# Loads of a table and of raw weights moved behind a store, and fewer idle matmuls, in front of step B of an FFT and MLP kernel

## The chip, the cores and the metric

The kernel runs on one core of a Trainium2 chip. The metric is the device time of one execution in microseconds (us), as the median of several runs. A core has five engines that work at the same time and wait for one another by semaphores: TensorE (PE in the profile, PEld its weight loads), VectorE (DVE), ScalarE (ACT), GpSimd (POOL) and SyncE (SP). SP, ACT and POOL also issue transfers (DMA). An instruction queue is worked off in order, so an issue that waits holds up those behind it. Queue 1 of the DMA carries what SP issues, queue 0 what POOL issues, queue 10 what ACT issues; all of them run on the same 16 DMA engines.

## The reference

The input `x` is 4 batches of 3008 tokens with 256 channels. Each batch goes through a Fourier transform over the tokens, a complex 256 x 256 mix with bias, a soft threshold, and the inverse transform. All 12032 tokens then go through a layer of 2048 hidden units with a leaky ReLU of its own slope for each unit.

```python
X = np.fft.rfft(x, axis=1)
Yr = Xr @ w_r - Xi @ w_i + b_r
Yi = Xr @ w_i + Xi @ w_r + b_i
Yr = np.sign(Yr) * np.maximum(np.abs(Yr) - lam, 0.0)
Yi = np.sign(Yi) * np.maximum(np.abs(Yi) - lam, 0.0)
y = np.fft.irfft(Yr + 1j * Yi, n=3008, axis=1)
...
h = y.reshape(12032, 256) @ w_in
g = np.maximum(h, 0.0) + alpha * np.minimum(h, 0.0)
return (g @ w_out).astype(np.float32)
```

`w_in` and `w_out` come as 64-bit floats. The kernel loads their raw words and converts each number on the chip into a high and a low 32-bit part (the `conv` steps).

## The kernel before

The transform of 3008 = 47 x 64 points is split. **Step A** (`a_load`, `a_mm`, `a_evac`) does the 47-point transforms as matmuls with the table `lf_s`: 16 groups `g` to a batch, two of them to a load. For batch 0 the result stays in SBUF as `a0_s`; for later batches `a_evac` copies it to a staging tile `ast` and puts a store to the DRAM buffer `ad` on a list, which `put()` issues on SP. **Step B** (`b_load`, `b_mm`, `b_evac`) takes the 24 slots of the first frequency index in 12 pairs `q`. `b_load(q)` rearranges pair `q` into a tile `bt` (three buffers); for batch 0 it copies from SBUF to SBUF by two transfers on POOL's queue. `b_mm(q)` multiplies with slots 2q and 2q+1 of the table `rb_s`. **The mix** (`m_mm`, `m_evac`) multiplies with the mixing weights `wr_s` and `wi_s`, **step C** (`c_mm`, `c_evac`) does the inverse 64-point part and stores to the buffer `zd`, and **step D** (`d_load`, `d_step`) the inverse 47-point part. What step D gives goes into the layer's two products (`l1_step`, `l2_step`, later `s_l1`, `s_l2`).

Nothing moves instructions but the program itself: each engine and each queue does its work in the order in which the code calls it (`tc.manual_schedule()`), and semaphores are set between engines where data or a buffer is passed on.

Batch 0's steps A to D stand alone at the start, up to about 104 us; there is no other work for TensorE yet. The steps of batches 1 to 3 are woven into the layer's products later. At the start SP issues, in order: batch 0's input (`x`), slots 0 to 3 of `rb_s`, the first input of batch 1 (`xt`), the mixing weights (`wm_f`), slots 4 to 11 of `rb_s`, and two loads of raw expert weights (`conv_load`, into `cw_s`). A loop over `seq` then does step A for batch 0's 16 groups and for batch 1's first 4 (the variable `EARLY`). In it, at `n == NG` (behind batch 0's last group), POOL is given `b_load` for q = 0, 1 and 2 (six transfers) and then `split_mix`: ScalarE writes the high parts of the mixing weights, and POOL behind its six issues the low parts (L142). Behind the loop come `put()`, which issues the four stores of batch 1's groups on SP, two small loads (`rd_s`, `alpha_s`), and `keep_warm(WARM)`: matmuls on a tile of zeros whose results nobody reads.

The loop over `t` then runs step B, the mix and step C in a pipeline. In round `t` TensorE has `b_mm(t)`, `m_mm(t-1)` and `c_mm(t-3)`; POOL has `b_load(t+3)`, which needs `b_mm(t)` to have freed the buffer, then the two negations of `X(t)` (L450, in `b_evac2`), which the `wi_s` matmuls of `m_mm(t)` read. `pump(PT[t])` puts in so many steps of the conversion of the raw weights. `m_evac(0)` writes its first result into the buffer `Yc`, one of the four in which batch 1's first groups wait for their stores.

Of the kernel before, what the change touches and what calls it, by code (L numbers as in the profile page):

```python
# [93 lines left out]
def fft_mix_moe(ctx, tc, x, w_r, w_i, b_r, b_i, w_in, w_out, alpha, la, rb, lc, rd, lf, cf, sel, out):  # L94
# [72 lines left out]
    def half(h):  # L167
        t = const.tile([128, 2, FH * 2 * C], F32R, tag=f"half{h}", name=f"w{h}")
        wi_h[h] = t[:, 0].rearrange("p (w k f) -> p w k f", w=2, k=CT)
        wo_h[h] = t[:, 1].rearrange("p (m w f) -> p m w f", w=2, f=C)  # L170

    def load_tables():
        nc.sync.dma_start(out=rd_s, in_=rd)
        nc.sync.dma_start(out=alpha_s, in_=alpha.rearrange("(k p) -> p k", p=128))
# [31 lines left out]
    def load_mix(*tags):  # L206
        for w, tag in zip((w_r, w_i), tags):
            t = work.tile([128, CT, C], F32, tag=tag, name="wm_f", bufs=1 if tag[1] in "tc" else None)
            nc.sync.dma_start(out=t, in_=w.rearrange("(k p) f -> p k f", p=128))
            mix_w.append(t)  # L210

    def load_rb(n0, n1):
        nc.sync.dma_start(out=rb_s[:, n0:n1], in_=rb[:, n0:n1])
# [10 lines left out]
    def split_mix():  # L224
        for t, w in zip(mix_w, mix):
            split(t, w[:, 0], w[:, 1], A, G)
        mix_w.clear()
# [24 lines left out]
    def conv_load():  # L252

        m, i = divmod(conv_m[0], 2)
        conv_m[0] += 1
        k = conv_m[0] % 3
        raw = cw_s[:, NSLOT + 8 * k:NSLOT + 8 * k + 8].rearrange("p (k n) f -> p k (n f)", k=2)
        raw = raw.rearrange("p k (n w) -> p k n w", w=2)
        src = w_out.bitcast(U32)[256 * m:256 * m + 256] if i else w_in.bitcast(U32)[:, 512 * m:512 * m + 512]
        nc.sync.dma_start(out=raw.rearrange("p k n w -> p k (n w)"), in_=src.rearrange("(k p) f -> p k f", p=128))  # L260
        conv_raw.append((raw, m, i))
# [48 lines left out]
    def pump(n):  # L310

        while n > 0:
            if not conv_ops:
                conv_fetch()
                second = conv_second(*conv_old.pop()) if conv_old else []
                first = conv_first(*conv_raw.pop(0)) if conv_raw else []
                first, second = ([(op,) for op in ops] for ops in (first, second))
                if first and second:
                    conv_ops.extend([second[0] + first[0], first[1], second[1], second[2] + second[3] + first[2]])
                else:  # L320
                    conv_ops.extend(first + second)
                if not conv_ops:
                    return
            for op in conv_ops.pop(0):
                op()
            n -= 1
# [5 lines left out]
    def put(*queues):  # L332
        for n, (o, i) in enumerate(stores):
            (queues or (nc.sync,))[n % max(len(queues), 1)].dma_start(out=o, in_=i)
        stores.clear()
# [44 lines left out]
    def a_mm(b, g):  # L380
        ps = ps_f.tile([NQ, 2, C], F32, tag="f", name="ps_a")
        pa[b, g] = ps
        if b < 2:
            ts = x_rows(b, g)
            n = 2 // len(ts)
            for i, t in enumerate(ts):
                PE.matmul(ps[:, n * i:n * i + n], lf_s, t, start=True, stop=True)  # L387
            return
        hi, lo = xp.pop((b, g))
        PE.matmul(ps, la_s[:, 0], hi, start=True, stop=False)  # L390
        PE.matmul(ps, la_s[:, 1], hi, start=False, stop=False)
        PE.matmul(ps, la_s[:, 0], lo, start=False, stop=True)

    def a_evac(b, g):
        ps = pa.pop((b, g))
        if b == 0:
            st = a0_s[:, g]
        else:
            tag = A1_TAGS[g] if b == 1 and g < len(A1_TAGS) else "zst"
            st = work.tile([NQ, 2, C], F32, tag=tag, name="ast", bufs={"bt": 3, "Yt": 1, "Yc": 1}.get(tag))  # L400
        if b == 0 and g % 2:
            V.tensor_copy(out=st, in_=ps)
        else:
            A.activation(out=st, in_=ps, func=AF.Copy)
        if b:
            stores.append((ad[b][:, 2 * g:2 * g + 2], st))
# [3 lines left out]
    def b_load(b, q):  # L410
        t = work.tile([128, 2, C], F32, tag="bt", name="bt", bufs=3)
        if b == 0:
            src = a0_s.rearrange("(w s q) g r c -> q w s (g r) c", w=4, s=2)[q]
        else:
            src = ad[b].rearrange("(w s q) r c -> q w s r c", w=4, s=2)[q]

        for k in range(2):
            (nc.gpsimd if b == 0 else nc.sync).dma_start(out=t[:, k], in_=src[:, k])
        bt[b, q] = t
# [546 lines left out]
    NG = R // 2  # L966
    EARLY = 4
    FILL = 14
    C0 = 2
    PT = [1, 2, 3, 3, 3, 3, 3, 3, 3, 3, 4, 4]  # L970
    TAIL = [['f', 1], ['ce', 3], ['me', 1], ['cm', 2], ['f', 1], ['ce', 2], ['cm', 1], ['ce', 1], ['d'], ['f', 2], ['e'], ['f', 6]]
    WARM = 70
    A1_TAGS = ("zst", "zst", "Yt", "Yc", "bt", "bt", "bt", "Xh", "Xl", "Xh", "Xl", "zst", "zst", "Yc")
    X1_TAGS = {4: ("Yl", "Yl"), 5: ("os", "Yt"), 6: ("gh",) * 4}
    idle = const.tile([128, 128], BF16, name="idle")
# [1 line left out]
    def keep_warm(n):  # L977
        ps = ps_f.tile([128, 512], F32, tag="f", name="ps_idle")
        for _ in range(n):
            PE.matmul(ps[:, 0:128], idle, idle, start=True, stop=True)  # L980

    with tc.manual_schedule():
# [8 lines left out]
        for g in range(EARLY // 2):  # L991
            a_load(1, g)
        load_mix("Yh", "Yh")
        load_rb(4, 12)
        conv_tags.update(v1=("yh", "yl"), ex=("xh", "xh"), lf=("xl", "xl"))
        for _ in range(C0):
            conv_load()
        seq = [(0, g) for g in range(NG)] + [(1, g) for g in range(EARLY)]

        for n, (b, g) in enumerate(seq):  # L1000
            a_mm(b, g)
            if n >= 1:
                a_evac(*seq[n - 1])
            if n == NG:
                for q in range(3):
                    b_load(0, q)
                split_mix()
                bias_parts()
        a_evac(*seq[-1])
        half(0)  # L1010
        put()
        load_tables()
        keep_warm(WARM)

# [13 lines left out]
        for t in range(NPAIR + 1):  # L1028
# [8 lines left out]
            if t < NPAIR:  # L1037
                pump(PT[min(t, len(PT) - 1)])
            if t in (2, 5):
# [152 lines left out]
        for k in range(len(spairs) + SLAG):  # L1192
# [9 lines left out]
            if k >= SLAG:  # L1202
                n, t = spairs[k - SLAG]
# [43 lines left out]
```

## Time and profile before

| what | value |
|---|---|
| time, median of 3 runs | 1356.6 us (1356.08 to 1357.65) |
| time of the profiled execution | 1356.09 us |
| its span (first to last instruction) | 1354.3 us |
| TensorE busy | 1339.6 us, 99% of the span |
| VectorE, ScalarE, POOL busy | 1037.7, 759.2, 379.5 us |
| chain that ended last | 96% on TensorE, 1% each on VectorE, ScalarE and DMA |

The span leaves out 1.8 us of the execution around the instructions. Busy time is a sum over the whole span; where an engine waits is seen in its timeline alone, which gives the start, the length and, in brackets, the idle time ahead of an instruction with what ended it. A row of a timeline merges like instructions that follow each other (xcount).

### The profile page before, as it was taken

The page shows a single profiled execution, that of the slowest core. Times are in us where ns is not written, and L with a number is a line of the kernel's source. Part 1 is how long each engine was busy: PE and PEld are TensorE (multiplying, and loading weights), DVE is VectorE, ACT ScalarE, POOL GpSimd, SP SyncE. Part 2 cuts the span into 40 slices and gives each one's busy share as a digit, 9 for nine tenths or more (in the row PEclk, how much of TensorE's full clock was granted, in tenths as well). Part 3 has the DMA queues.
Part 4 walks back from the last instruction along what each step waited for, and adds up shares of the span by engine and source line. Part 5 has one row for each costly group of instructions (what it writes and reads, how often), then busy time and mean ns, then how long its engine had stood idle before and what let it go on. Part 6 is the DMA issues. An engine that isn't in the chain of part 4 may idle for free.

```text
span 1354.3 us, 25104 instructions
## 1 busy us (share of the span) xinstructions
PE 1339.6 (99%) x9208; PEld 1252.3 (92%) x9208; DVE 1037.7 (77%) x1931; ACT 759.2 (56%) x1528; POOL 379.5 (28%) x403
## 2 busy tenths in 40 slices
PE   9999999999999999999999999999999999999998
PEld 5979989999999999999999999999999999999998
DVE  2766866777777777776768888888888888888885
ACT  3566645665566655545556555555565556555553
POOL 3854742221322232222212211122112111221222
PEclk9999999999999999999999999999999999999999
DMA  9964223342334312111110110111011101110001
GB/s 238 261 173 152 82 94 98 103 136 85 97 97 129 98 64 81 45 59 47 36 36 1 40 28 2 39 28 27 6 36 28 28 6 36 29 28 8 21 17 28
DMA packets 88119, 89.66 MB, mean 66 GB/s; under 512 B 42318, under 2 KB 70449, under 8 KB 87996
## 3 DMA queue, kind: packets, MB, share of 16 engines
q1 hardware_dynamic: 79428, 76.76, 19.9%
q0 software_dynamic: 5168, 8.02, 2.3%
q10 hardware_dynamic: 3399, 3.27, 0.8%
q8 instruction: 73, 1.20, 0.4%
q14 instruction: 51, 0.41, 0.1%
HBM read 50.49 MB, written 34.34 MB: 63 GB/s over the span
## 4 chain that ended last, share of the span: by engine, by line
PE 96%; DVE 1%; DMA 1%; issue 1%; ACT 1%; POOL 0%; ACTq 0%; DVEq 0%
PE ps_h L785 24%; PE ps_h L680 14%; PE ps_m L486 6%; PE ps_o L887 6%; PE ps_o L888 6%; PE ps_o L886 6%; PE ps_d L611 4%; PE ps_o L718 3%; PE ps_o L717 3%; PE ps_o L719 3%; PE ps_b L426 3%; PE ps_m L473 3%; PE ps_a L387 2%; PE o_last L719 2%; PE o_last L717 2%; PE o_last L718 2%
## 5 line engine op out<-in xcount | busy, mean ns | idle before, releaser
L785 PE MATMUL ps_h<-yh,w 128*128 128x512 f32 (+1 forms) x960 | 315.6, 390 | 0.0
L824 POOL TENSOR_TENSOR l<-t,h 128x512 fp32r<-128x512 f32 x98 | 127.0, 1296 | 496.6 <-ACT h L822 456.7
L785 PEld LDWEIGHTS ps_h<-yh,w 128*128 128x128 f32 x960 | 180.0, 188 | 33.2
L789 DVE SCALAR_TENSOR_TENSOR sq<-sq,beta_s,ps_h 128x512 f32<-128x512 f32 (+1 forms) x240 | 168.0, 733 | 55.0 <-ACT sq L788 54.2
L680 PE MATMUL ps_h<-yh,w 128*128 128x384 f32 (+1 forms) x704 | 206.2, 335 | 2.7 <-DVE q L687 2.7
L785 PE MATMUL ps_h<-yl,w 128*128 128x512 f32 (+1 forms) x480 | 186.3, 388 | 0.0
L691 ACT ACTIVATE gh<-q 128x384 fp32r<-128x384 f32 (+1 forms) x192 | 99.1, 516 | 148.6 <-DVE q L687 147.5
L687 DVE SCALAR_TENSOR_TENSOR q<-q,beta_s,ps_h 128x384 f32<-128x384 f32 (+1 forms) x192 | 115.5, 601 | 79.9 <-ACT q L686 78.1
L692 POOL TENSOR_TENSOR gl<-q,gh 128x384 fp32r<-128x384 f32 (+1 forms) x90 | 96.6, 1073 | 267.0 <-ACT gh L691 259.5
L804 ACT ACTIVATE dh<-sq 128x768 fp32r<-128x768 f32 x112 | 94.8, 846 | 118.0 <-DVE sq L789 72.8
L788 ACT ACTIVATE sq<-ps_h 128x512 f32<-128x512 f32 (+1 forms) x240 | 133.1, 586 | 27.5 <-PE ps_h L785 23.0
L680 PEld LDWEIGHTS ps_h<-yh,w 128*128 128x128 f32 x704 | 129.3, 189 | 5.7 <-DVE q L687 2.2
L822 ACT ACTIVATE h<-t 128x512 fp32r<-128x512 f32 x98 | 62.0, 633 | 104.5 <-DVE t L820 101.2
L680 PE MATMUL ps_h<-yl,w 128*128 128x384 f32 (+1 forms) x352 | 116.5, 331 | 0.0
L686 ACT ACTIVATE q<-ps_h 128x384 f32<-128x384 f32 (+1 forms) x192 | 91.4, 476 | 35.5 <-PE ps_h L680 34.2
L719 PE MATMUL ps_o<-w,gl 128*128 128x256 f32 x384 | 107.9, 281 | 1.7 <-POOL gl L692 1.7
L718 PE MATMUL ps_o<-w,gh 128*128 128x256 f32 x384 | 108.3, 282 | 0.0
L717 PE MATMUL ps_o<-w,gh 128*128 128x256 f32 x384 | 107.9, 281 | 0.0
L785 PEld LDWEIGHTS ps_h<-yl,w 128*128 128x128 f32 x480 | 90.5, 189 | 13.6
L819 DVE TENSOR_TENSOR dl<-sq,dh 128x768 fp32r<-128x768 f32 x98 | 93.4, 954 | 3.8 <-ACT dh L804 3.6
L888 PE MATMUL ps_o<-l,sw_a 128*128 128x256 f32 x294 | 82.0, 279 | 0.0
L886 PE MATMUL ps_o<-h,sw_a 128*128 128x256 f32 x294 | 81.9, 279 | 0.0
(211 smaller groups left out, 3625.6 us busy)
## 6 DMA issues: line engine op xcount, KB each, us to landing
zt<-zd SPq DMA_DIRECT2D x32, 384.0 KB
ad<-ast SPq DMA_DIRECT2D x48, 192.0 KB
bt<-ad SPq DMA_DIRECT2D x72, 128.0 KB
zd<-zst SPq DMA_DIRECT2D x36, 256.0 KB
xt<-in_x SPq DMA_DIRECT2D x21, 320.0 KB
out<-oT SPq DMA_DIRECT2D x152, 32.0 KB
cw_s<-in_moe_w_in SPq DMA_DIRECT2D x8, 512.0 KB
cw_s<-in_moe_w_out SPq DMA_DIRECT2D x8, 512.0 KB
```

What stands on the lines that cost most here:

```text
L680: PE.matmul(ps, wi_h[m // FH][:, w, ct, 128 * (m % FH):128 * (m % FH) + 128], a[:, ct, 0:n], start=(k == 0), stop=(k == 3 * CT - 1))
L687: V.scalar_tensor_tensor(out=q, in0=q, scalar=beta_s[:, m:m + 1], in1=ps, op0=ALU.mult, op1=ALU.add)
L691: A.activation(out=hi, in_=q, func=AF.Copy)
L717: PE.matmul(a, hi[:, t], w[:, 0], start=(i, k) in first, stop=False)
L718: PE.matmul(a, hi[:, t], w[:, 1], start=False, stop=False)
L719: PE.matmul(a, lo[:, t], w[:, 0], start=False, stop=(i, k) in last)
L785: PE.matmul(ps, wi_h[m // FH][:, w, ct, 128 * (m % FH):128 * (m % FH) + 128], a[:, ct, 0:w1], start=(k == 0), stop=(k == 3 * CT - 1))
L788: A.activation(out=q[:, j], in_=ps, func=AF.Relu, scale=-1.0)
L789: V.scalar_tensor_tensor(out=q[:, j], in0=q[:, j], scalar=beta_s[:, m:m + 1], in1=ps, op0=ALU.mult, op1=ALU.add)
L824: G.tensor_tensor(out=l24, in0=t24, in1=f(h24), op=ALU.subtract)
L886: PE.matmul(o, wh, gh, start=first, stop=False)
L888: PE.matmul(o, wh, gl, start=False, stop=last)
```

## The change

Three loads leave their place on SP ahead of step A's loop. At `n == NG + 1`, when batch 1's group 0 is on the list of stores, `put()` now issues this one store; behind it stand the first raw load, slots 4 to 11 of the table, and the second raw load. `WARM` falls from 70 to 20, and the first round of step B puts in no step of the conversion (`PT[0]` from 1 to 0).

```diff
-    PT = [1, 2, 3, 3, 3, 3, 3, 3, 3, 3, 4, 4]
+    PT = [0, 2, 3, 3, 3, 3, 3, 3, 3, 3, 4, 4]
...
-    WARM = 70
+    WARM = 20
...
         load_mix("Yh", "Yh")
-        load_rb(4, 12)
         conv_tags.update(v1=("yh", "yl"), ex=("xh", "xh"), lf=("xl", "xl"))
-        for _ in range(C0):
-            conv_load()
         seq = [(0, g) for g in range(NG)] + [(1, g) for g in range(EARLY)]
 
         for n, (b, g) in enumerate(seq):
...
                 split_mix()
                 bias_parts()
+            if n == NG + 1:
+                put()
+                conv_load()
+                load_rb(4, 12)
+                for _ in range(C0 - 1):
+                    conv_load()
         a_evac(*seq[-1])
```

On SP, from the mixing weights (`wm_f`) on, the issues stand as follows; a row with - stands there before alone, one with + after alone.

```order
 L209 DMA wm_f<-in_w_r 128x2x256
 L209 DMA wm_f<-in_w_i 128x2x256
+L334 DMA ad_158<-ast 96x512
+L260 DMA cw_s<-in_moe_w_in 128x2x512
 L213 DMA rb_s<-tab_rb 128x1024
-L260 DMA cw_s<-in_moe_w_in 128x2x512
-L260 DMA cw_s<-in_moe_w_out 128x2x512
-L334 DMA ad_158<-ast 96x512 x4
+L260 DMA cw_s<-in_moe_w_out 128x2x512
+L334 DMA ad_158<-ast 96x512 x3
```

The table's slots and the two raw loads (`cw_s`) went from the place behind the mixing weights to the place behind the first of the four stores (`ad`); the other three stores, `rd_s` and `alpha_s` have three transfers more ahead of them than before.

On ScalarE, from the second split of a mixing weight to the second round of step B, there stood before (`Xh` is `b_evac`'s copy, L273 a conversion's first step, L499 is in `m_evac(0)`):

```order
L139 ACTIVATE wi_s<-wm_f 128x512
L404 ACTIVATE ast<-ps_a 96x512 x4
L440 ACTIVATE Xh<-ps_b 128x4x128
L273 ACTIVATE conv<-cw_s 128x512
L440 ACTIVATE Xh<-ps_b 128x4x128 x2
L499 ACTIVATE Yc<-ps_m,lam_s 128x512
L273 ACTIVATE conv<-cw_s 128x512
```

and there stands now:

```order
L139 ACTIVATE wi_s<-wm_f 128x512
L404 ACTIVATE ast<-ps_a 96x512 x4
L440 ACTIVATE Xh<-ps_b 128x4x128 x2
L273 ACTIVATE conv<-cw_s 128x512
L440 ACTIVATE Xh<-ps_b 128x4x128
L499 ACTIVATE Yc<-ps_m,lam_s 128x512
L273 ACTIVATE conv<-cw_s 128x512
```

The first step of the conversion, which reads the first raw load, went from between the first two `Xh` copies to behind both, and the steps that follow it are each a little later in the rounds.

## Rows read from the trace of the kernel before

**Rows 1.** Chain that ended last, 20 to 105 us: start us, us, what
```profile
20.99 2.08 POOL bt L418 x3
...
23.07 8.02 DMA bt<-a
...
31.14 0.71 PE ps_b L426 x4
...
32.28 3.05 PE ps_m L473 x24
...
104.12 0.93 PE ps_d L611 x8
```

**Rows 2.** TensorE's timeline: start us, us, engine line op out<-in form xcount
```profile
1.00 4.02 PE L980 MATMUL ps_idle<-idle 128*128 128x128 bf16 x36 [1.00 <-DVE idle L986]
...
23.29 1.10 PE L387 MATMUL ps_a<-xt,lf_s 94*96 94x512 f32 x2 [1.11 <-ACT ast L404]
...
24.23 4.07 PE L980 MATMUL ps_idle<-idle 128*128 128x128 bf16 x70
...
29.46 2.38 PE L426 MATMUL ps_b<-rb_s,bt 128*128 128x128 f32 x16 [1.17 <-issue]
...
33.02 0.40 PE L473 MATMUL ps_m<-wi_s,Xh 128*128 128x256 f32 x2
...
33.26 0.28 PE L473 MATMUL ps_m<-wi_s,Xl 128*128 128x256 f32 x1
...
35.16 1.06 PE L426 MATMUL ps_b<-rb_s,bt 128*128 128x128 f32 x8
...
44.77 1.05 PE L426 MATMUL ps_b<-rb_s,bt 128*128 128x128 f32 x8
```

**Rows 3.** Timeline of all engines, POOL's rows (a row merges neighbours)
```profile
20.99 4.10 POOL L418 DMA_DIRECT2D bt<-a  x6 [15.91 <-DVE bias_h L199]
...
26.42 1.26 POOL L142 TENSOR_TENSOR wi_s<-wm_f,wi_s 128x512 fp32r<-128x512 f32 x1
...
30.89 1.37 POOL L418 DMA_DIRECT2D bt<-a  x2 [3.21 <-PE ps_b L426]
...
32.29 0.41 POOL L450 TENSOR_SCALAR Xh<-Xh 128x256 fp32r<-128x256 f32 x1
...
32.66 0.41 POOL L450 TENSOR_SCALAR Xl<-Xl 128x256 fp32r<-128x256 f32 x1
...
33.66 1.37 POOL L418 DMA_DIRECT2D bt<-a  x2
```

**Rows 4.** `bt`'s issue at 20.99 on POOL, time to landing
```profile
DMA to landing us min/median/max: 8.4/8.4/8.4
```

**Rows 5.** DMA queues, 22 to 23 us: packets, MB, share of 16 engines
```profile
q1 hardware_dynamic: 165, 0.40, 101.7%
```

**Rows 6.** DMA queues, 25 to 26 us
```profile
q0 software_dynamic: 156, 0.18, 99.9%
...
q1 hardware_dynamic: 54, 0.09, 28.5%
```

**Rows 7.** Timeline of all engines, ScalarE's first split of a mixing weight
```profile
21.40 0.63 ACT L139 ACTIVATE wr_s<-wm_f 128x512 fp32r<-128x512 f32 x1 [2.03 <-DMA wm_f<-in_w_r]
```

**Rows 8.** SP's queue, timeline of its issues
```profile
16.77 0.38 SPq L213 DMA_DIRECT2D rb_s<-tab_rb  x1
...
18.98 0.37 SPq L260 DMA_DIRECT2D cw_s<-in_moe_w_out  x1
...
23.26 5.42 SPq L334 DMA_DIRECT2D ad<-ast  x4
```

**Rows 9.** DMA issues, 1 to 2 us: KB each, median us to landing
```profile
lf_s<-tab_lf POOLq DMA_DIRECT2D x1, 35.2 KB, 2.8
```

**Rows 10.** SP's queue, 25 to 26.5 us
```profile
24.43 2.31 SPq L334 DMA_DIRECT2D ad<-ast  x1
```

**Rows 11.** `bt`'s issues from 33.66 on, time to landing
```profile
DMA to landing us min/median/max: 9.6/10.0/10.3
```

## The prediction

> **What bounds the kernel now.** I read the page first: TensorE is busy nearly all of the span, so a change saves time only where TensorE stands still or does work that is not wanted. Then I read the chain of work that ended last, in order of time, around the edit [rows 1]. There the reader is to see that TensorE is not the link between step A and step B. The chain goes from the third `bt` issue on POOL's queue into a transfer that takes 8.02 us, lands at 31.09, and releases the second half of `b_mm(1)` at 31.14. From there to the end of step B, and on through the fill work to step D's first matmul at 104.12, the chain lies on TensorE almost without a break. So about 8 us ahead of step B are set by a transfer, and all later work hangs on it.
>
> TensorE's timeline shows the same from its side [rows 2]. Step A ends at 24.39. The 70 idle matmuls run from 24.23 to 28.30. `b_mm(0)` starts at 29.46, so there is a hole of 1.17 us even behind the idle matmuls. The idle matmuls are therefore no cost of their own: they fill a wait for `bt`.
>
> Why is `bt` late? By its landing row the first transfer takes 8.4 us from its issue at 20.99 [rows 3, 4], so it lands at 29.4, just ahead of `b_mm(0)`. The queue rows show what the engines did instead. Between 22 and 23 us queue 1 (SP's) has 101.7% of the 16 DMA engines and moves 0.40 MB, and queue 0 (POOL's, which carries `bt`) has no row at all [rows 5]. Between 25 and 26 us queue 0 has 99.9% and queue 1 is down to 28.5% [rows 6]. What queue 1 carries from about 21.4 on is known from the order of SP's issues: `w_r`'s load released ScalarE at 21.40 [rows 7], and behind the two mixing loads stand slots 4 to 11 of the table (issued at 16.77) and two raw weight loads, the last issued at 18.98 [rows 8]. Each of the three is 128 x 1024 words of 4 bytes, 1.57 MB together. At 0.40 MB in 1 us they are 3.9 us of all DMA engines: the stretch from 21.4 to about 25.
>
> **The change, part by part.**
>
> *Three transfers go behind the first store.* They now stand on SP behind the store of (1, 0), which SP issues at 23.26 [rows 8], as it waits for ScalarE's copy of that group. ScalarE's copies, TensorE's matmuls of step A and the issues on POOL stand as before. All six `bt` issues lie on POOL between 20.99 and 25.09 [rows 3], and the four of `bt(0)` and `bt(1)` are ahead of the first moved transfer. So the 3.9 us of foreign work in front of them go. Estimate: `bt(0)` lands at 29.4 - 3.9 = 25.5, the second half of `bt(1)` at 31.1 - 3.9 = 27.2. The bounds: nothing (if `bt` is slow by itself), and, from the other side, the 2.8 us that the small load of `lf_s`, POOL's first, took from issue to landing [rows 9]; that would put `bt(0)` at 24 to 24.5. I take the middle one, since the queue rows show the very stretch.
>
> *50 idle matmuls fewer.* 4.07 us for 70 is 0.058 us each, so the 20 that stay end at about 28.30 - 2.9 = 25.4. This alone gains nothing, for `b_mm(0)` waited until 29.46; but with 70 it could not have started before 28.3. Together the two edits let `b_mm(0)` start at about 25.5, 3.9 us earlier.
>
> *What is late next.* The stall goes to POOL. Its queue is in order: six `bt` issues, the two low parts of the mixing weights until 26.42 + 1.26 = 27.68, then `bt(3)`'s two issues (1.37 us), then the two negations of `X(0)` [rows 3]. In the trace `bt(3)` starts at 30.89, when `b_mm(0)` has freed its buffer. After the change it can start at 27.68 and no earlier: 3.21 us gained, not 3.9. The negated halves are used by the `wi_s` matmuls of `m_mm(0)`. The high half was ready at 32.70 for a matmul at 33.02 (0.32 us of slack), the low half at 33.07 for one at 33.26 (0.19 us) [rows 2, 3]. TensorE may use up the smaller slack, so these matmuls move by 3.21 + 0.19 = 3.4 us. From there TensorE runs without a gap into `b_mm(2)`, from 35.16 to 31.8.
>
> *Costs at nothing, and their covers.* `b_mm(2)` needs the moved table slots, now due at 31.8. Issued behind the store and one raw load at about 24.5, they have 1.25 MB to go through queue 1, store, raw load and themselves (96 x 512, 128 x 1024 and 128 x 1024 words); at 0.40 MB per us that needs 3.1 us of engines shared with `bt(2)`; I expect them at 29 to 31. One us of cover is thin. The first raw load is wanted by ScalarE's conversion, whose first step now stands behind the second `Xh` and not between the first two; the next ScalarE operation for which TensorE waits is `Xh(2)`, 4 us later, so a late raw load costs nothing below that. The conversion is one of its steps behind at the end of step B, and the drain of the tail carries that step out while TensorE has fill work until step D. The other three stores, `rd`, `alpha` and the third raw load on SP get later by the three transfers that now stand ahead; the store out of `Yc` must land before ScalarE overwrites that buffer in `m_evac(0)`, and ScalarE has 3 us or more there before `Xh(3)`.
>
> *Sum.* The profiled execution took 1356.1 us; minus 3.4 is 1352.7. It ran 0.5 us under the median of the three runs (1356.6), so the median of the changed kernel should be 1353.2, 0.25% less.
>
> **A rule against it.** The Trainium skill, "DMA: Bandwidth & Descriptors", section "Queues, rings and completion order", says that each DMA engine goes round robin between the queues that have work for it, a packet at a time. By that rule queue 0 would have had its turns from 22 us on whatever queue 1 held, and moving queue 1's work would help little; what that would give is rival 3. The row of 22 to 23 us shows no packet of queue 0 beside a full queue 1, so here the trace does not bear the rule out for the start of a transfer; in the row of 25 to 26 both move.
>
> **The rivals.**
>
> 1. *The table comes late.* For it: while `bt` flows, an issue on SP can take 2.31 us [rows 10] where others take 0.38 [rows 8]. If store, raw load and table each take that, the table's issue ends at 23.26 + 3 x 2.31 = 30.2; its data takes 1.3 us at 0.40 MB per us and twice to three times that if it shares the engines, so it lands at 31.5 to 34, up to 2.2 us behind 31.8. The gain shrinks to between 1.2 and 2.7 us: 1353.9 to 1355.4 on the median's scale, on which the rivals below stand too. Against it: the long issues end when `bt` is through, and that is earlier now.
>
> 2. *The gain is given back in step B.* `bt(4)` was the tightest transfer of the step: its second half took 10.3 us from its issue at 34.34 (two issues of 0.68 us from 33.66), landed at 44.65 and was used at 44.77 [rows 2, 11]. Its issue now comes some 3.2 us earlier. If the DMA engines have the same work ahead of it as before, it lands at 44.6 again, and 3.3 of the 3.4 us are lost: 1356.5. Against it: most of what stood ahead of it on queue 1 (`alpha`, the third raw load, the next slots) is issued later relative to it.
>
> 3. *The change does not free `bt`.* Later `bt` transfers take long too. If the first ones take 8.4 us for themselves, `b_mm(0)` stays at 29.46 and nothing is gained. TensorE would then stand still from 25.4 on for 4 us. The first idle matmuls, which follow on nothing, took 4.02 us for 36, 0.112 us each [rows 2], twice the 0.058 of the later ones: by their length the lower of the two levels of the clock, 1.2 of 2.4 GHz. If the clock falls in the hole, a like stretch of 4 us at the lower level loses 2 us: 1356.6 to 1358.6. Against it: the row with queue 1 alone.
>
> 4. *The table comes so late that the kernel is slower.* It decides from a landing at 35.2, where `b_mm(2)` stood. If the issue comes at 30.2, as in rival 1, and the landing takes 8.4 us as `bt`'s did, `b_mm(2)` starts at 38.6, 3.4 us later than before: 1360.0. Against it: behind 30 us there is far less ahead of it in the queues than was ahead of `bt` at 21.
>
> **How the numbers follow.** A measurement of this kernel can tell some 0.2%, 2.7 us, from no change. The forecast (2.7 to 4 us gained) has 0.52, rival 1 0.18, rival 2 0.14, rival 3 0.08, rival 4 0.08. The forecast's own range is 1352.6 to 1353.9. Faster is the forecast alone, 0.52; same is rivals 1 and 2 and most of rival 3, 0.39; slower is rival 4 and a little of 3, 0.09. The range runs from 1352.0 (all 3.9 us gained against the profiled execution's own 1356.1, and 0.2 of scatter) to 1356.8, which takes in rivals 1 and 2 and leaves out 3 and 4.
>
> **What would show it.** Right: the first `bt` lands within 5 us of its issue; `b_mm(0)` starts near 25.5; `bt(3)` starts on POOL at 27.7; the `wi_s` matmuls of `m_mm(0)` are near 29.6 and wait for POOL; `b_mm(2)` is near 31.8; step D starts near 100.7. Wrong: `b_mm(0)` near 29 (rival 3); a wait of `b_mm(2)` for `rb_s` (1 and 4); a wait of `b_mm(4)` or a later one for `bt` (2). The forecast is wrong if step D starts less than 2.7 us earlier.

## The result, and the profile after

| | before | after |
|---|---|---|
| median, us (range) | 1356.34 (1355.21 to 1357.65, 6 runs) | 1364.35 (1362.52 to 1368.46, 5 runs) |
| ratio to before, 95% interval | 1 | 1.0060 [1.0048, 1.0071] |
| profiled execution, us; its span | 1356.1; 1354.3 | 1363.2; 1361.5 |
| end of step A; first matmul of step D, us | 24.39; 103.96 | 24.97; 111.11 |
| step D to the end of the span, us | 1250.3 | 1250.4 |

The changed kernel is slower by 8 us; 3.4 us faster was forecast. A sixth run of after, 1455.17 us at a granted clock of 0.849, is left out, here and in the ratio; with it the median is 1365.33. From step D on the two profiled executions take the same time, so in them all of the loss lies between 24 and 111 us.

TensorE's timeline of the kernel after, to be read against [rows 2]:

```profile
24.81 1.28 PE L980 MATMUL ps_idle<-idle 128*128 128x128 bf16 x20
25.93 1.11 PE L426 MATMUL ps_b<-rb_s,bt 128*128 128x128 f32 x8
28.34 0.68 PE L426 MATMUL ps_b<-rb_s,bt 128*128 128x128 f32 x4 [1.30 <-DMA bt<-a]
30.30 0.71 PE L426 MATMUL ps_b<-rb_s,bt 128*128 128x128 f32 x4 [1.28 <-DMA bt<-a]
...
32.70 0.63 PE L473 MATMUL ps_m<-wi_s,Xh 128*128 128x256 f32 x2
...
35.85 1.06 PE L426 MATMUL ps_b<-rb_s,bt 128*128 128x128 f32 x8
...
43.62 0.50 PE L466 MATMUL ps_m<-bias_p,ones 4*128 4x512 f32 x1 [2.34 <-DVE Y L500]
...
92.82 0.50 PE L466 MATMUL ps_m<-bias_p,ones 4*128 4x512 f32 x1 [1.44 <-DVE Y L500]
...
111.11 3.89 PE L611 MATMUL ps_d<-rd_s,zt 96*128 96x94 f32 x32
```

The reader is to see three things. `b_mm(0)` does start 3.5 us earlier (25.93 for 29.46). The gain is gone at once: `b_mm(1)` waits twice for its own `bt`, the pair of `wi_s` and `Xh` takes 0.63 us where it took 0.40, and `b_mm(2)` is at 35.85, where it was at 35.16. And two waits follow that the prediction did not have, ahead of 43.62 and of 92.82.

The granted clock by stretches, in the kernel after (columns: stretch, its length, busy us of PE, PEld, DVE, ACT and POOL with their instructions, PEclk, DMA share, GB/s):

```profile
28.00:31.00 3.00, 1.38 (x9) 1.10 (x9) 0.40 (x1) 0.00 (x0) 2.77 (x6) 1.00 1.03 233
31.00:35.00 4.00, 4.00 (x19) 3.75 (x19) 1.12 (x2) 1.29 (x2) 2.14 (x4) 0.57 1.05 283
...
45.00:49.00 4.00, 4.00 (x22) 3.95 (x21) 3.90 (x7) 1.78 (x3) 3.54 (x6) 0.57 0.80 222
```

Before, these stretches stood at 1.00. TensorE had been busy for 1.38 of 3 us when the clock fell to about its lower level (1.2 of 2.4 GHz), and again after it stood still for 2.34 us ahead of 43.62. By an estimate from these rows, 4 us at 0.57 are some 1.7 us of work lost each time.

SP's queue in the kernel after, against [rows 8, 10]:

```profile
23.85 0.33 SPq L334 DMA_DIRECT2D ad<-ast  x1
24.22 1.23 SPq L260 DMA_DIRECT2D cw_s<-in_moe_w_in  x1
25.50 1.96 SPq L213 DMA_DIRECT2D rb_s<-tab_rb  x1
27.50 1.50 SPq L260 DMA_DIRECT2D cw_s<-in_moe_w_out  x1
29.10 2.85 SPq L334 DMA_DIRECT2D ad<-ast  x3
...
32.53 0.47 SPq L174 DMA_DIRECT2D alpha_s<-in_moe_alpha  x1
33.33 8.35 SPq L260 DMA_DIRECT2D cw_s<-in_moe_w_in  x1
```

The three moved issues take 1.2 to 2.0 us each, and the stores behind them are done being issued at 31.95 instead of 28.68. ScalarE's timeline of the kernel after shows what waits for that (round 2), and a second thing at the end of step B (rounds 10 and 11):

```profile
42.09 0.69 ACT L499 ACTIVATE Yc<-ps_m,lam_s 128x512 f32<-128x512 f32 x1 [4.50 <-DMA ad<-ast]
...
88.70 0.64 ACT L282 ACTIVATE w<-conv 128x512 fp32r<-128x512 f32 x1 [3.41 <-DVE conv L288]
...
96.24 0.63 ACT L282 ACTIVATE w<-conv 128x512 fp32r<-128x512 f32 x1 [3.65 <-DVE conv L288]
```

Both lie on the chain that ended last, which runs over TensorE almost alone in [rows 1]:

```profile
30.81 11.26 DMA ad<-ast
...
94.54 1.67 DVE conv L288
```

`Yc` is the buffer out of which the fourth store reads: the relu of `m_evac(0)` overwrites it and has to wait until the store has landed. The chain spends 11.26 us in that store. Between the two the chain runs for some 18 us in two stores of step C's results; TensorE's timeline has no wait from 44 to 91 us. The waits at L282 are ScalarE's for VectorE's step of the weight conversion. Before, VectorE did in round 10:

```profile
79.27 0.68 DVE L446 TENSOR_TENSOR Xl<-ps_b,Xh 128x512 fp32r<-128x512 f32 x1
79.86 0.68 DVE L288 SCALAR_TENSOR_TENSOR conv<-cw_s,conv 128x512 uint32<-128x512 uint32 x1
```

and ScalarE followed:

```profile
80.58 0.63 ACT L282 ACTIVATE w<-conv 128x512 fp32r<-128x512 f32 x1 [1.39 <-DVE conv L288]
```

A group is one of the steps that `pump` puts in; four groups make a whole turn of the conversion, which finishes one block of raw weights and begins the next. After, one group late, the last group of the turn before stands between the two (L291 and L275 on VectorE, L292 on GpSimd):

```profile
85.16 0.68 DVE L446 TENSOR_TENSOR Xl<-ps_b,Xh 128x512 fp32r<-128x512 f32 x1
85.76 0.68 DVE L291 TENSOR_TENSOR conv<-conv,w 128x512 f32<-128x512 f32 x1
86.36 0.62 DVE L275 TENSOR_SCALAR conv<-conv 128x512 uint32<-128x512 uint32 x1
87.02 1.64 DVE L288 SCALAR_TENSOR_TENSOR conv<-cw_s,conv 128x512 uint32<-128x512 uint32 x1
```

L288 does not only start later, it also takes 1.64 us instead of 0.68. GpSimd's part of the late group runs beside it, and where GpSimd has nothing to do, at 102.23, L288 takes 0.69 us in the same place behind L275 (POOL's row, then VectorE's):

```profile
86.67 1.43 POOL L292 TENSOR_TENSOR w<-conv 128x512 fp32r<-128x512 f32 x1
...
101.78 0.42 DVE L275 TENSOR_SCALAR conv<-conv 128x512 uint32<-128x512 uint32 x1
102.23 0.69 DVE L288 SCALAR_TENSOR_TENSOR conv<-cw_s,conv 128x512 uint32<-128x512 uint32 x1
```

Behind L282 in ScalarE's order stand the copies of step C (L561), their stores and the next relu (L499), for which TensorE waits. So the loss has three candidates: the store out of `Yc`, the clock, and the place of the conversion's groups within the last rounds.

### The profile page after: what moved, and what is told of

It reads as the page before. It is cut to its first block, busy times and chain, and to the rows that moved or that the text cites. A ratio compares the mean times of both kernels' runs of the same rounds, so it can differ in the third digit from the quotient of the medians.

```text
span 1361.5 us, 25002 instructions
## 1 busy us (share of the span) xinstructions
PE 1339.8 (98%) x9158; PEld 1252.1 (92%) x9158; DVE 1036.0 (76%) x1931; ACT 759.3 (56%) x1528; POOL 379.3 (28%) x403
## 3 DMA queue, kind: packets, MB, share of 16 engines
q0 software_dynamic: 5168, 8.02, 2.2%
q8 instruction: 72, 1.18, 0.4%
## 4 chain that ended last, share of the span: by engine, by line
PE 92%; DMA 3%; DVE 2%; ACT 1%; issue 1%; SPq 0%; ACTq 0%; POOL 0%; DVEq 0%
PE ps_h L785 24%; PE ps_h L680 14%; PE ps_m L486 6%; PE ps_o L887 6%; PE ps_o L888 6%; PE ps_o L886 6%; PE ps_d L611 4%; PE ps_o L718 3%; PE ps_o L717 3%; PE ps_o L719 3%; PE ps_b L426 2%; PE ps_a L387 2%; PE o_last L719 2%; PE o_last L717 1%; PE o_last L718 1%; PE o_last L886 1%
## 5 line engine op out<-in xcount | busy, mean ns | idle before, releaser
L788 ACT ACTIVATE sq<-ps_h 128x512 f32<-128x512 f32 (+1 forms) x240 | 133.1, 586 | 27.2 <-PE ps_h L785 22.7
```

What stands on the lines that cost most here:

```text
L788: A.activation(out=q[:, j], in_=ps, func=AF.Relu, scale=-1.0)
```

## The experiments

All were timed beside the kernel before. "A to D" is from the end of step A to step D's first matmul, "11 to D" from the first matmul of `b_mm(11)` to there, both from the profiled execution's TensorE timeline; step A's own end varies from 23.9 to 26.7 from run to run, in the order of before (24.4 to 26.2) as in the others.

| run | median, us | ratio [95%] | A to D | 11 to D |
|---|---|---|---|---|
| before | 1356.3 to 1357.4 | 1 | 79.6 | 22.6 |
| after | 1364.35 | 1.0060 [1.0048, 1.0071] | 86.1 | 25.1 |
| e1_yl | 1363.72 | 1.0049 [1.0037, 1.0061] | 88.5 | 28.6 |
| e2_warm70 | 1361.82 | 1.0035 [1.0022, 1.0047] | 86.8 | 28.9 |
| e3_yl_warm70 | 1365.02 | 1.0058 [1.0046, 1.0070] | 89.3 | 28.5 |
| e4_before_warm20 | 1359.25 | 1.0015 [1.0006, 1.0023] | 83.1 | 22.6 |
| e5_pt03 | 1359.91 | 1.0025 [1.0015, 1.0035] | 80.7 | 22.6 |
| e6_before_pt0 | 1360.52 | 1.0036 [1.0020, 1.0052] | 85.1 | 28.2 |
| e7_pt03_yl | 1358.87 | 1.0015 [1.0007, 1.0024] | 79.4 | 22.6 |
| e8_pt03_yl_warm70 | 1357.22 | 1.0011 [0.9999, 1.0022] | 83.4 | 22.6 |
| e9_tables | 1357.42 | 0.9996 [0.9984, 1.0009] | 79.9 | 22.6 |
| e10_rb_first | 1357.51 | 1.0000 [0.9989, 1.0011] | 80.6 | 22.6 |
| e11_rb_tables | 1356.86 | 0.9991 [0.9981, 1.0002] | 78.4 | 22.6 |
| e12_rb_tables_warm70 | 1358.46 | 1.0002 [0.9990, 1.0014] | 81.5 | 23.4 |
| e13_pt_r10 | 1363.01 | 1.0047 [1.0033, 1.0061] | 83.2 | 24.8 |
| e14_pt_r9 | 1360.59 | 1.0021 [1.0013, 1.0030] | 82.6 | 23.0 |
| e15_before_ahead | 1359.12 | 1.0018 [1.0004, 1.0032] | 79.0 | 22.6 |

A single profile can stand 2.7 to 3.8 us off its kernel's median (1363.2 beside 1360.52 in e6, 1361.0 beside 1357.22 in e8), so below the traces say what happens and the ratios say what it is worth (0.0010 is 1.4 us).

### The front: the buffer and the idle matmuls

**e1_yl**, the kernel after with the fourth store out of another buffer:

```diff
-    A1_TAGS = ("zst", "zst", "Yt", "Yc", "bt", ...
+    A1_TAGS = ("zst", "zst", "Yt", "Yl", "bt", ...
```

> The changed kernel, but batch 1's fourth staged group lies in a buffer of tag Yl, which nobody wants until round 7, and no longer in Yc. The order of all engines is the same. Buffer theory (ScalarE's first Yc copy waits for the fourth store, which landed near 42 us behind three moved loads, and TensorE stands still from 41.3 to 43.6 and then runs at the lower clock to 48.6): the copy follows Xh(2) near 37.6, m_mm(2) follows b_mm(3) without a gap, b_mm(4) comes near 45.7 instead of 49.4, step D near 107.6 instead of 111.3, time some 3.7 us below the changed kernel's 1363.2: 1359.5. Clock theory (the lower clock behind the missing idle matmuls is the loss): no more than 0.5 us better, 1363. Raw-load theory (ScalarE would next wait as long for a raw weight load): b_mm(4) stays within 1 us of 49.4.

**e2_warm70**, the kernel after with the idle matmuls of before, and **e3_yl_warm70** with both edits:

```diff
-    WARM = 20
+    WARM = 70
```

> The changed kernel with 70 idle matmuls again instead of 20. Buffer theory: the clock stays at its upper level from 31 to 35 us and b_mm(2) comes near 34.7 instead of 35.9, but the Yc copy still waits for the store that lands near 42, so b_mm(4) stays near 49.4 and the time within 1 us of 1363.2. Clock theory: without the low stretches the kernel gains 1.5 to 3 us, 1360 to 1361.7, and b_mm(4) comes as much earlier.

> The changed kernel with both edits: the fourth staged group in Yl, and 70 idle matmuls. Buffer theory with the clock as its second part: b_mm(2) near 34.7, no gap before m_mm(2), no low clock, b_mm(4) near 44.3, step D near 106: 1358, 5 us below the changed kernel and 1.5 above the kernel before, the rest being raw loads that come late in step B's last rounds. Clock theory alone: no better than with 70 idle matmuls alone. Buffer theory without the clock: the same as with Yl alone, 1359.5.

**e4_before_warm20**, the kernel before with 20 idle matmuls and nothing else (`WARM = 70` to `20`):

> The kernel before with 20 idle matmuls instead of 70, and nothing else. Clock theory: TensorE stands still from 25.4 to 29.5 us, the granted clock falls to 0.5 for about 3 us in m_mm(0), and all behind it is 1.5 us later: 1357.9. If the idle matmuls are no cover for the clock: no change, 1356.4.

In e1 the wait at L499 was gone; in e2 it was 2.24 us and held TensorE up no longer, and in e2 and e3 `b_mm(4)` was back at 44.9 and 44.5. Yet step D came no earlier than after's 111.1: from `b_mm(11)` on these three took 28.5 to 28.9 us, more than after's own 25.1. By the ratios e1 and e2 gave 1.5 and 3.4 us, but e3 with both edits is no better than after (1.0058 to 1.0060): in its profile ScalarE's L273 waits 7.29 us for a raw load at 49.66. So the store and the clock are real waits, their gains do not add up, and a large part of the loss lies behind them; a theory that held only these two fell here. e4 shows the cost of fewer idle matmuls alone. TensorE's timeline of e4:

```profile
29.88 3.75 PE L426 MATMUL ps_b<-rb_s,bt 128*128 128x128 f32 x16 [4.20 <-issue]
...
38.90 1.05 PE L426 MATMUL ps_b<-rb_s,bt 128*128 128x128 f32 x8
```

and its clock by stretches:

```profile
28.00:31.00 3.00, 1.12 (x5) 1.15 (x6) 0.00 (x0) 0.00 (x0) 0.00 (x0) 0.50 1.02 254
31.00:35.00 4.00, 4.00 (x17) 3.34 (x16) 1.39 (x3) 1.76 (x3) 2.75 (x6) 0.50 0.77 150
```

After 4.2 us without work `b_mm(0)` and `b_mm(1)` take 3.75 us instead of 2.38, and `b_mm(2)` is 3.7 us later than in [rows 2]; the ratio says 2.0 us. In the kernel before, the idle matmuls hold the clock up.

### The conversion's place

**e5_pt03**, the kernel after with 3 groups in round 1, and **e6_before_pt0**, the kernel before without the group of round 0:

```diff
 (e5, against after)
-    PT = [0, 2, 3, 3, 3, 3, 3, 3, 3, 3, 4, 4]
+    PT = [0, 3, 3, 3, 3, 3, 3, 3, 3, 3, 4, 4]
 (e6, against before)
-    PT = [1, 2, 3, 3, 3, 3, 3, 3, 3, 3, 4, 4]
+    PT = [0, 2, 3, 3, 3, 3, 3, 3, 3, 3, 4, 4]
```

> The kernel after with one entry of the list of conversion groups changed: round 1 takes 3 groups where it takes 2, so that from round 1 on the conversion of the raw expert weights stands where the kernel before has it (1, 3, 6, 9 ... groups done), and round 0 still has none. Nothing else is moved. Theory 1 (phase of the conversion): with the conversion one group behind, ScalarE's copy at L282 waits 3.4 to 3.7 us for VectorE's L288 in each of rounds 10 and 11 where the kernel before waits 1.4 and 0.9 there, and the relu and the stores of step C stand behind it. Then from the first matmul of b_mm(11) to the first of step D it goes back to 22 to 23.5 us (25.1 in the kernel after, 22.6 before), the two waits at L282 are at most 1.5 us, and the median falls by 2 to 5 us to 1360 to 1363; the start of step B (b_mm(4) near 49) stays late. Rival (the raw loads come too late because SyncE's queue is held up, whatever the table says): the waits stay above 3 us and the median stays within 1 us of 1365.

> The kernel before with one entry of the same list changed: round 0 takes no conversion group where it takes 1, as in the kernel after; loads, idle matmuls and buffers as before. Theory 1 (phase of the conversion): the front of step B is as before (b_mm(4) near 44.8), the waits at L282 in rounds 10 and 11 are 3.4 to 3.7 us, b_mm(11) to step D takes 26 to 29 us, and the median is 4 to 7 us above the kernel before, 1360 to 1363. Rival (late loads alone): within 1 us of before, 1355.5 to 1357.5, with waits of 1.5 us or less at L282.

Both came out as theory 1, the place of the conversion, had it (e5 0.1 us below its range), and the rival of late loads fell. ScalarE's L282 in rounds 10 and 11 of e5:

```profile
85.68 0.63 ACT L282 ACTIVATE w<-conv 128x512 fp32r<-128x512 f32 x1 [1.39 <-DVE conv L288]
91.00 0.63 ACT L282 ACTIVATE w<-conv 128x512 fp32r<-128x512 f32 x1 [0.96 <-DVE conv L288]
```

and of e6, where nothing but one number differs from the kernel before:

```profile
86.99 0.63 ACT L282 ACTIVATE w<-conv 128x512 fp32r<-128x512 f32 x1 [3.63 <-DVE conv L288]
94.52 0.63 ACT L282 ACTIVATE w<-conv 128x512 fp32r<-128x512 f32 x1 [3.63 <-DVE conv L288]
```

Part of this price is again the clock. TensorE's wait in round 11 of e6, and the stretch from 90 to 104 us:

```profile
91.12 0.79 PE L466 MATMUL ps_m<-bias_p,ones 4*128 4x512 f32 x1 [2.90 <-DVE Y L500]
...
90.00:104.00 14.00, 11.63 (x44) 8.76 (x45) 7.59 (x12) 6.58 (x12) 6.22 (x6) 0.76 0.46 142
```

Before and after stand at 1.00 in this stretch. In e1, e2 and e3 the same wait is 2.99 to 3.05 us, and in the 2 us behind it the clock is 0.50; in after's profile the wait is 1.44 us and the clock stays up. With that goes 11 to D, 28.2 to 28.9 us in these four and 25.1 in after. The profiled execution of after is one of its two fastest: at a mean granted clock of 0.997 it took 1363.24 us and another run 1362.52, while two runs at 0.995 took 1366.31 and 1368.46.

By the ratios the group is worth 4.7 us in the kernel after (1.0060 to 1.0025) and 4.9 us in the kernel before (1 to 1.0036). It could still be the place of the groups in the last rounds, raw loads that come a round later before that, or the one group more that the tail has to drain. **e13_pt_r10** and **e14_pt_r9** put the group back only late, in the kernel after, and **e15_before_ahead** shifts the kernel before the other way:

```diff
 (e13)
+    PT = [0, 2, 3, 3, 3, 3, 3, 3, 3, 3, 5, 4]
 (e14)
+    PT = [0, 2, 3, 3, 3, 3, 3, 3, 3, 4, 4, 4]
 (e15)
+    PT = [1, 3, 3, 3, 3, 3, 3, 3, 3, 3, 4, 4]
```

> The kernel after with the missing conversion group put back only in round 10 (5 groups instead of 4), so that the first group of round 10 still stands one late and round 11 is as in the kernel before. If it is the place of the groups within rounds 10 and 11 that costs: the wait at L282 for L288 stays at 3.4 us or more in round 10 and is at most 1.6 us in round 11, and about half of the 5.4 us that the group in round 1 gave back is had: 1361.5 to 1363.5. If it is only the one group left over for the tail: all of it, 1359 to 1361.

> The kernel after with the missing group put back in round 9 (4 groups instead of 3): rounds 1 to 8 stand one group late as in the kernel after, rounds 10 and 11 as in the kernel before. If only the places in rounds 10 and 11 cost: the waits at L282 there are at most 1.6 us and the median is that of the kernel with 3 groups in round 1 (1359.9), 1359 to 1361. If the lateness in rounds 1 to 8 costs as well (raw loads one round later, behind the loads of the next batch's rows on SyncE's queue): 1362 to 1364.5.

> The kernel before with one conversion group more in round 1, so that from there on the conversion is one group ahead of where it is; loads, buffers and idle matmuls as before. If the cost of a shift comes from where L288 and L282 fall within a round, a shift the other way changes the waits too: with L288 done in the round before, the 1.4 and 0.9 us waits in rounds 10 and 11 go and the median is 1354 to 1356.5. If the waits only move to the raw weights (L273, whose transfers are then due earlier): 1356.5 to 1360.

L282 in rounds 10 and 11 of e13:

```profile
86.40 0.64 ACT L282 ACTIVATE w<-conv 128x512 fp32r<-128x512 f32 x1 [3.62 <-DVE conv L288]
91.70 0.64 ACT L282 ACTIVATE w<-conv 128x512 fp32r<-128x512 f32 x1 [1.39 <-DVE conv L288]
```

One long wait stays and one goes, and e13's ratio lies between those of after and e5, though the tail has the amount of before. Its interval overlaps both of theirs, so what speaks against the amount in the tail is the wait, and 11 to D, which is 24.8. In e14 both waits are short (1.38 and 1.18), and it is within the interval of e5. So it is the place in rounds 10 and 11, where four groups, a whole turn, are done per round; lateness in rounds 1 to 8 costs nothing that the intervals show. e15 was slower by 0.18%, as its second branch had it: L273 waited 2.0 us for a raw load at 77.7, but 11 to D stayed at 22.6, and its profile loses 2 us behind step D's start. That part was not followed up.

### What is left: the queue on SP

With the conversion in place, **e7_pt03_yl** (e5 and e1's buffer) and **e8_pt03_yl_warm70** (70 idle matmuls as well):

> The kernel after with both edits, the 3 groups in round 1 and the fourth store of the next batch out of buffer Yl where it is out of Yc, so that the relu of round 2 waits for no store. 20 idle matmuls stay. Theory: the wait at L499 (4.5 us) and those at L282 are gone; what is left is the lower clock between 31 and 38 us (b_mm(2) 37.5 and b_mm(4) 47.1 with the other buffer alone, 35.2 and 44.8 before). Step D at 106 to 107.5, median 1358 to 1360.5. If the buffer did not matter beside the phase: the same as with the table alone. If neither matters: 1364 to 1365.

> The kernel after with three edits: 3 groups in round 1, the fourth store out of Yl, and 70 idle matmuls as before; so the only differences to the kernel before are the three moved loads and the group that round 0 does not do. Theory: nothing of the three losses is left. b_mm(0) 28.7, b_mm(2) 34.5 to 35.2, b_mm(4) 44.3 to 44.9, step D at 103.3 to 104.5, median 1355.5 to 1357.5: what the earlier table gives (0.7 us at b_mm(0)) and no more. If the moved raw loads cost something of their own (the third one is held 5 to 8 us on SyncE's queue), conversions late in rounds 4 to 6 show waits for the raw weights at L273 and the median is 1358 to 1362.

e7 has 1358.87, so the buffer is worth 1.4 us beside e5 (1.0025 to 1.0015) and 1.5 in e1 beside after; both times the intervals overlap. Its table came late: `b_mm(2)` waited 2.59 us for `rb_s` and started at 35.20. e8, in which of the change the moved loads are left (and the group of round 0, done in round 1, and the other buffer), cannot be told from before by its interval, but its profile has the cost that was named: at 50.65 ScalarE's L273 waited 8.23 us for the third raw load, which SP issued from 39.05 to 45.26. In e7 the issue was held too. SP's queue in e7:

```profile
34.10 0.46 SPq L174 DMA_DIRECT2D alpha_s<-in_moe_alpha  x1
34.60 7.00 SPq L260 DMA_DIRECT2D cw_s<-in_moe_w_in  x1
```

Queue 1 of the kernel after, 38 to 40 us and then 40 to 42 (packets, MB, share of 16 engines):

```profile
q1 hardware_dynamic: 1131, 0.23, 77.0%
...
q1 hardware_dynamic: 976, 0.11, 48.0%
```

By their sizes in the trace some 1880 of these 2107 packets are of 4 bytes, and the held issue ends at 41.68, when most of them are through. `alpha` is 8 KB, read as 128 x 16 words, no two adjacent. The Trainium skill, "DMA: Bandwidth & Descriptors", section "Rules for kernel authors", says that a last dimension that is not contiguous becomes one descriptor for each element; the number of 4-byte packets agrees. **e9_tables** issues `rd` and `alpha` behind the third raw load, **e10_rb_first** puts the table ahead of the first raw load, **e11_rb_tables** does both, and **e12_rb_tables_warm70** is e11 with 70 idle matmuls; all stand on e7:

```diff
 (e9)
         put()
-        load_tables()
         keep_warm(WARM)
...
                 load_rb(2 * t + 8, 2 * t + 14)
+            if t == 2:
+                load_tables()
 (e10)
                 put()
+                load_rb(4, 12)
                 conv_load()
-                load_rb(4, 12)
```

> The kernel with 3 conversion groups in round 1 and the fourth store out of Yl (20 idle matmuls), and the small tables rd and alpha issued after the third raw load and the second rb transfer of round 2 instead of ahead of them. Theory A (alpha's transfer of 4-byte pieces fills SyncE's queue, so the raw load behind it is held): the third raw load, held 7.0 us from 34.6 on without this edit, is issued in under 3 us, the waits of ScalarE at L273 for raw weights (2.1, 3.1 and 2.7 us near 39, 45 and 52) fall below 1 us, and the median goes to 1356.5 to 1358 from 1358.9. Theory B (it is held by the bytes queued ahead of it, 512 KB three times and three stores): the hold stays at 5 us or more, only earlier, and the median stays within 1 us of 1358.9.

> The same kernel (3 groups in round 1, Yl, 20 idle matmuls; tables where they were) with the later slots of step B's table ahead of the first raw load, both still behind the first store. In the kernel without this edit b_mm(2) waited 2.6 us for the table and started at 35.2, at full clock. Theory: the table lands 1.6 to 2.5 us earlier, b_mm(2) starts at 31.8 to 33.5 and the median falls by 1 to 3 us, to 1356 to 1358, unless the first raw load, now later, makes ScalarE wait longer at L273 in round 1 (2.4 us there now). Rival: b_mm(2) starts earlier, but the gathers of bt(3) and bt(4) or the raw weights take it back, median within 0.7 us of 1358.9.

> Both edits, table of step B ahead of the first raw load and rd and alpha behind the third. If the prediction's 3.4 us from fewer idle matmuls are to be had at all, they are here: b_mm(2) at 31.8 to 33, step D at 101 to 103 (before 104.0), median 1353.5 to 1356. If the front of step B is bound by what its transfers bring, not by when TensorE is free: b_mm(4) at 44 to 45 as before, D at 103.5 to 105, median 1356 to 1358.

> The same with 70 idle matmuls, so that the 50 are told apart with all else equal. If they are worth the 3.4 us of the prediction: 2.5 to 4 us above the kernel with 20. If they lie under the gathers or are given back: within 1 us of it, b_mm(0) near 28.7 and b_mm(4) within 0.5 us of that kernel's. If they hold the clock up: 1 us or more faster than the kernel with 20.

SP's queue in e9:

```profile
31.98 0.52 SPq L260 DMA_DIRECT2D cw_s<-in_moe_w_in  x1
...
36.31 0.37 SPq L174 DMA_DIRECT2D alpha_s<-in_moe_alpha  x1
42.06 3.85 SPq L260 DMA_DIRECT2D cw_s<-in_moe_w_out  x1
```

The third raw load takes 0.52 us, and now the fourth is held, again the next one behind `alpha`. So theory A is right about the hold; it moved by one load, and ScalarE's waits for raw weights stayed at 1.7 and 3.0 us, not below 1. By the ratio e9 is 2.6 us faster than e7. e10 gained 2.0 us by its ratio, though in its profile `b_mm(2)` was no earlier: TensorE stood still for 1.65 of 3 us from 28 on, and the clock was 0.50 from 31 to 37. e11 is the fastest of the study by its ratio, 0.9991 [0.9981, 1.0002], and cannot be told from the kernel before. TensorE's timeline in e11:

```profile
28.32 0.68 PE L426 MATMUL ps_b<-rb_s,bt 128*128 128x128 f32 x4 [0.26 <-DMA bt<-a]
29.16 0.71 PE L426 MATMUL ps_b<-rb_s,bt 128*128 128x128 f32 x4 [0.16 <-DMA bt<-a]
...
33.92 1.13 PE L426 MATMUL ps_b<-rb_s,bt 128*128 128x128 f32 x8 [0.57 <-DMA rb_s<-tab_rb]
```

Counted from the end of its step A, which was 1.6 us late, `b_mm(2)` comes 2.9 us earlier than before, `b_mm(4)` 2.7, but step D only 1.2: at 52.5 ScalarE waits 3.47 us for the raw load that `alpha` held. So most of the prediction's 3.4 us can be had at the front, and more than half of it is given back later. e12 is 1.5 us behind e11 by the ratios, with intervals that overlap: in this arrangement doing without the 50 matmuls is worth 1.5 us, if anything, and all of the change together 1.2 us against the kernel before, if anything, not 3.4.

## Why the prediction was wrong

- *Three transfers go behind the first store*: the first half held. The two transfers of `bt(0)` took 3.6 and 3.4 us from their issues at 21.42 and 22.10 and landed at 25.0 and 25.5, as estimated; `b_mm(0)` came at 25.93 behind the idle matmuls. (The 8.02 us of [rows 1] are those of the fourth issue, not the third; the sum does not hang on it.) `bt(1)` was mis-sized: its second half landed at 30.3 instead of 27.2. The moved transfers went out from 24.2 on and shared the engines with it, as the queues of the kernel after show (23 to 24 us, where queue 1 has no row, then 28 to 29; packets, MB, share of 16 engines):

```profile
q0 software_dynamic: 126, 0.15, 49.5%
...
q1 hardware_dynamic: 91, 0.17, 48.0%
q0 software_dynamic: 76, 0.12, 44.6%
```

- *50 idle matmuls fewer*: the end of the 20 was right (25.9 for 25.4), but they were counted as a gain without a price. TensorE then had 1.3 us of waiting twice, and the clock fell. This is rival 3's mechanism, though `bt` was freed. Alone it cost 2.0 us in the kernel before (e4); put back into the kernel after, it gave 3.4 us (e2), but nothing beside the other buffer (e3) and nothing that can be told in e8 and e12.
- *What is late next*: POOL did as said, `bt(3)` was issued at 28.06 for 27.68. But the `wi_s` matmuls of `m_mm(0)` were at 32.70, not 29.6, as `b_mm(1)` stood ahead of them; `b_mm(2)` came at 35.85 instead of 31.8.
- *Costs at nothing, and their covers* is the step that failed and made a loss of it. "The conversion is one of its steps behind at the end of step B, and the drain of the tail carries that step out" priced an amount of work and not its place. It is one group behind, and in rounds 10 and 11 that puts two VectorE instructions in front of the one that ScalarE waits for, and a GpSimd instruction beside it: 4.7 to 4.9 us with the lower clock that follows in some profiles, shown both ways (e5, e6) and pinned to these rounds (e14, with e13's waits). "ScalarE has 3 us or more there before `Xh(3)`" was to cover a store that took 11.26 us from its issue to its landing: 4.5 us of waiting in the profile, 1.4 us in the ratios.
- The three moved loads alone, with all this put right (e8), cost nothing that can be told: 0.11%, with an interval from -0.01 to 0.22%. They gain nothing that can be told either.
- *The rule against it*: once both queues have packets they share about evenly, 48.0 to 44.6% in the last two rows. That fits the Trainium skill, "DMA: Bandwidth & Descriptors", section "Queues, rings and completion order", by which an engine goes round robin between the queues that have work. [rows 5] showed a start that queue 0 lost altogether, and the prediction took that for the whole; it did not ask what the moved transfers would do to `bt(1)`. A part of that row is no loss at all: in the kernel after, with five packets of queue 1 in all from 22 us on, queue 0's first packet came only behind 22.7, 1.3 us after the first issue. Before, it came no earlier than 23.8, 2.8 us after, so the full queue 1 may account for some 1.5 us of the start, not for all of it.
- Rival 1's late table was seen where the rest was mended (e7, 2.59 us), rival 2's give-back too (e11), there through the raw weights; in e12 `b_mm(4)` did wait 1.04 us for `bt`.

Not settled: what sets the size of the clock's part from run to run, and how much of the 4.7 to 4.9 us it is. That 4.7, 1.4 and 2.0 us come to the 8 us lost proves little, as in e3 the gains do not add up. In e7 TensorE stood still from 33 to 35 us and the clock stayed at 1.00.

## What to carry to other kernels

When a step of background work is shifted, look at where its pieces fall between the foreground instructions of an in-order engine, in the rounds with least slack, at what runs beside them, and not only at how much of it is left. When transfers are put behind others, look at everything that the queue issues after them, down to the store whose buffer somebody overwrites. Idle matmuls that cover a wait may also hold the clock: taking them away can cost if the wait stays in any part.

## What the hardware showed

- An 8 KB load in 4-byte pieces held the next issue on its queue for 7.0 and 8.35 us (e7, after), until most of its 4-byte packets (2048 words) were through; behind fewer transfers, in the kernel before, the next issue took 1.70 us. Moved by one load, it held the next one (3.85 us, e9).
- Two queues with packets shared the engines about evenly (48.0% and 44.6%, after). A queue 0 that starts had its first packet 1.3 us after the issue beside an almost empty queue 1 (after) and at least 2.8 us after it beside a full one (before).
- The same VectorE instruction (L288) took 0.69 us with GpSimd idle (102.23, after) and 1.64 us with a GpSimd instruction beside it (87.02, after), both times directly behind L275.
- TensorE's granted clock was 0.50 for some us behind a wait of 2.90 to 3.05 us (e6, e1, e2, e3) and stayed at 1.00 behind one of 1.44 (after), but also through 2 us without work (e7).
